# Two of 112 zero fills move to the GpSimd queue, in parts for four, one and eleven DMA engines

## The chip, the cores and the metric

The kernel runs on 1 core of one Trainium2 chip. The metric is the device time of one execution in microseconds (us), lower is better. Three runs of the kernel before took 810.0, 810.16 and 810.81 us; their median is 810.16 us.

## The reference

One decode step of a transformer block and its gradients: a layer norm, attention of one query token with 16 heads over the last 4096 positions of a key cache and a value cache (8 groups of heads, 32768 positions, 256 wide), and a bilinear gated feed-forward layer. What is returned is the block's output and the gradients of the input, of both caches and of five weight matrices. Only the last W = 4096 positions of the caches take part:

```python
W = min(4096, max(256, Sk // 4))                    # Sk = 32768
k = jnp.repeat(k_cache[:, :, Sk - W:, :], rep, axis=1)
v = jnp.repeat(v_cache[:, :, Sk - W:, :], rep, axis=1)
...
_out, _vjp = jax.vjp(_f, A_x, A_k_cache, A_v_cache, A_wq, A_wo, B_w_gate, B_w_up, B_w_down)
_grads = _vjp(grad_out)
return (_out0, *[jnp.asarray(_g) for _g in _grads])
```

The gradients of the two caches (`out_2` for keys, `out_3` for values, each 1 x 8 x 32768 x 256 in bf16) are therefore zero in their first 28672 positions. Those zeros are 224 MB (235 million bytes) of the 280.59 MB that the kernel writes to device memory.

## The kernel before, in words

**Arithmetic.** Phase one goes over the eight groups g: `scores(g)` transposes the keys and makes the softmax weights, `moments(g, p_f)` multiplies keys and values into sums. A middle part of small matrix-vector steps does the output projection, the feed-forward layer and its gradient. Phase two goes over the eight groups again, makes the gradients of keys and values of the last 4096 positions (`d_ps`, L579, copied out in L583 to L587), stores them, and makes the weight gradients in between. Tile schedules the instructions of each engine and places the waits.

**Loads and stores.** `LD` is the ScalarE queue (ACT): it issues the later loads of the caches and weights and all stores of results. `ZQ` is the SyncE queue (SP): it issues the first loads (L92 to L185), and after them nothing but zero fills. GpSimd (POOL) issues no transfer at all in this kernel; it sets a part of the tile `zeros` (L55) and makes two identity matrices, all in the first 4.3 us.

**Zero fills.** The tile `zeros` holds 128 partitions x ZW = 8192 bf16 zeros, so one row is 16,384 bytes. The 224 MB are cut into 112 regions of 128 rows, 2 MB each, and each region is one transfer (L187 to L202):

```python
fills += [reg[i] for i in range(NZ)]                # NZ = 7, 16 times
zsem = [tc.alloc_semaphore(f"zsem{j}") for j in range(DEEP)]
for i, reg in enumerate(fills):
    if i >= DEEP:                                   # DEEP = 8
        tc.keep_in_program_order(ZQ.wait_ge(zsem[i % DEEP], 16 * (i // DEEP)))
    fill = ZQ.dma_start(out=reg, in_=zeros[:])
    ...
    tc.keep_in_program_order(fill.then_inc(zsem[i % DEEP], 16))
for j in range(DEEP):
    filled = tc.keep_in_program_order(ZQ.wait_ge(zsem[j], 16 * len(range(j, len(fills), DEEP))))
```

Fill i is issued when fill i - 8 has landed, so eight of them are under way. The last loop (L200, L201) waits for the last eight fills, and the kernel ends behind it. The fills carry semaphores of their own, not Tile's.

**Packets and DMA engines.** The core has 16 DMA engines. The trace records each packet with its queue, size, start and time, but not with its engine. One row of a fill is one packet of 16,384 bytes, and a packet of 4 bytes (the completion mark) follows each eight rows: 112 fills x 16 = 1792 such marks belong to the fills. So each fill gives every engine eight rows. A packet starts within a few ns of the end of the packet before it on the same engine, so the packets can be strung into 16 chains, one per engine, which then carry no number but an end.

Of the kernel before, what the change touches and what calls it, by code (L numbers as in the profile page):

```python
# [15 lines left out]
G = 8  # L16
Dh = 256
W = 4096
# [4 lines left out]
Sk = 32768  # L23
EPS = 1e-5
SCALE = 1.0 / 16.0
ZW = 8192
NZ = (Sk - W) * Dh // (128 * ZW)
ZM = 5120
DEEP = 8
# [5 lines left out]
def kernel(  # L35
        ctx, tc, A_x, A_k_cache, A_v_cache, A_wq, A_wo, B_x, B_w_gate, B_w_up, B_w_down, grad_out,
           out_0, out_1, out_2, out_3, out_4, out_5, out_6, out_7, out_8):
    nc = tc.nc
    LD = nc.scalar
    ZQ = nc.sync  # L40
# [12 lines left out]
    zeros = const.tile([128, ZW], bf16)  # L53
# [133 lines left out]
    fills = []  # L187
    for g in range(G):
        for o in (out_2, out_3):
            reg = o[0, g, 0:Sk - W, :].rearrange("s d -> (s d)").rearrange("(n p f) -> n p f", p=128, f=ZW)  # L190
            fills += [reg[i] for i in range(NZ)]
    zsem = [tc.alloc_semaphore(f"zsem{j}") for j in range(DEEP)]
    for i, reg in enumerate(fills):
        if i >= DEEP:
            tc.keep_in_program_order(ZQ.wait_ge(zsem[i % DEEP], 16 * (i // DEEP)))
        fill = ZQ.dma_start(out=reg, in_=zeros[:])
        tc.info.no_tile_sem_insts.add(fill.ins.name)
        tc.add_to_no_dep_group("fills", fill.ins)
        tc.keep_in_program_order(fill.then_inc(zsem[i % DEEP], 16))
    for j in range(DEEP):  # L200
        filled = tc.keep_in_program_order(ZQ.wait_ge(zsem[j], 16 * len(range(j, len(fills), DEEP))))  # L201
    tc.declare_fence(filled.ins, group="fills")  # L202
# [437 lines left out]
```

## Time and profile before

| what | value |
|---|---|
| median of the runs | 810.16 us |
| the profiled execution | 810.97 us, span 808.1 us in the profile |
| DMA | 339.02 MB moved, 420 GB/s mean, "9" in tenths in 39 of 40 slices |
| SP's fills | 112 x 2048 KB, issued from 17.9 to 768.0 us |
| last wait for a fill over | 806.8 us |
| busiest engine, PE | 484.3 us, 60% of the span |
| GpSimd | 3.7 us busy, 9 instructions |

Times in the profile count from the first instruction of the span. "DMA share" in a table of windows is the mean busy share of the 16 DMA engines, so one engine alone gives 1/16 = 0.06. The DMA queues are named q1 (transfers that SP issued) and q10 (ACT); "instruction" rows are the engines' program code being fetched.

### The profile page before, as it was taken

The page shows a single profiled execution, that of the slowest core. Times are in us where ns is not written, and L with a number is a line of the kernel's source. Part 1 is how long each engine was busy: PE and PEld are TensorE (multiplying, and loading weights), DVE is VectorE, ACT ScalarE, POOL GpSimd, SP SyncE. Part 2 cuts the span into 40 slices and gives each one's busy share as a digit, 9 for nine tenths or more (in the row PEclk, how much of TensorE's full clock was granted, in tenths as well). Part 3 has the DMA queues.
Part 4 walks back from the last instruction along what each step waited for, and adds up shares of the span by engine and source line. Part 5 has one row for each costly group of instructions (what it writes and reads, how often), then busy time and mean ns, then how long its engine had stood idle before and what let it go on. Part 6 is the DMA issues. An engine that isn't in the chain of part 4 may idle for free.

```text
span 808.1 us, 8346 instructions
## 1 busy us (share of the span) xinstructions
PE 484.3 (60%) x3128; PEld 252.7 (31%) x3151; DVE 369.3 (46%) x1152; ACT 191.2 (24%) x301; POOL 3.7 (0%) x9
## 2 busy tenths in 40 slices
PE   3799999999999955119326664533674664230000
PEld 2454545455455532108313322211231221000000
DVE  3279356455536417881336545258843444540000
ACT  1521331322330102001014243221232343330000
POOL 1000000000000000000000000000000000000000
PEclk9899999999999976559858557555555557555555
DMA  9999999999999999999999999999999999999994
GB/s 371 396 427 429 429 429 428 430 428 427 431 430 426 422 426 429 431 432 426 425 420 423 427 436 427 413 421 429 428 429 426 428 431 429 429 429 427 430 428 196
DMA packets 24942, 339.02 MB, mean 420 GB/s; under 512 B 2755, under 2 KB 3398, under 8 KB 4422
## 3 DMA queue, kind: packets, MB, share of 16 engines
q1 hardware_dynamic: 17842, 254.96, 74.4%
q10 hardware_dynamic: 7060, 83.53, 24.4%
q8 instruction: 24, 0.39, 0.2%
q14 instruction: 16, 0.13, 0.0%
HBM read 57.89 MB, written 280.59 MB: 419 GB/s over the span
## 4 chain that ended last, share of the span: by engine, by line
DMA 24%; PE 12%; DVE 11%; ACT 2%; issue 1%; DVEq 0%; ACTq 0%
DMA out_dram<-arena 24%; PE d_ps L579 4%; PE rows_ps L251 3%; PE tr_ps L248 3%; DVE arena L417 2%; DVE arena L587 2%; DVE arena L586 2%; DVE arena L472 1%; PE dqb_ps L458 1%; DVE arena L502 1%; DVE arena L595 1%; ACT arena L584 1%; ACT arena L539 1%; DVE arena L392 1%; ACT arena L583 0%
## 5 line engine op out<-in xcount | busy, mean ns | idle before, releaser
L579 PE MATMUL d_ps<-arena,rT 32*128 32x512 bf16 x256 | 59.5, 564 | 129.9 <-DVE arena L587 101.3
L303 DVE TENSOR_SCALAR arena<-arena,p_f 128x256 bf16<-128x256 bf16 x512 | 109.7, 281 | 53.8 <-PE M_ps L307 29.0
L248 PE MATMUL tr_ps<-ident_bf,arena 128*128 128x128 bf16 x1024 | 102.5, 254 | 29.1 <-DVE arena L541 25.4
L307 PE MATMUL M_ps<-arena 128*128 128x512 bf16 x489 | 118.4, 380 | 1.4 <-issue 0.6
L248 PEld LDWEIGHTS <-arena 128*128 128x128 bf16 x1024 | 74.5, 113 | 90.7 <-issue 88.6
L251 PE MATMUL rows_ps<-arena,vpad 128*16 128x512 bf16 x256 | 96.0, 470 | 6.0 <-ACT arena L265 2.8
L265 ACT COPY arena<-tr_ps 128x1024 bf16<-128x1024 bf16 x64 | 61.7, 1015 | 119.1 <-PE tr_ps L248 119.1
L587 DVE CAST arena<-d_ps 128x512 bf16<-128x512 f32 x64 | 43.5, 680 | 56.2 <-DMA out_dram<-arena 56.2
L583 ACT CAST arena<-d_ps 128x512 bf16<-128x512 f32 x64 | 37.7, 588 | 126.1 <-PE d_ps L579 122.2
L579 PEld LDWEIGHTS <-rT 32*128 32x128 bf16 x256 | 12.4, 98 | 165.2 <-issue 83.5
L307 PEld LDWEIGHTS <-arena 128*128 128x128 bf16 x512 | 46.4, 98 | 52.3 <-issue 6.3
L586 DVE CAST arena<-d_ps 128x512 bf16<-128x512 f32 x64 | 44.0, 688 | 37.4 <-PE d_ps L579 37.3
L311 PE MATMUL ok_ps<-arena 128*16 128x256 bf16 x512 | 59.3, 273 | 1.1 <-DVE arena L292 0.9
L584 ACT CAST arena<-d_ps 128x512 bf16<-128x512 f32 x64 | 38.1, 595 | 64.4 <-DMA out_dram<-arena 64.4
L311 PEld LDWEIGHTS <-arena 128*16 128x16 bf16 x512 | 44.5, 90 | 14.7 <-issue 4.5
L539 ACT COPY arena<-tr_ps 128x1024 bf16<-128x1024 bf16 x32 | 32.8, 1026 | 16.0 <-PE tr_ps L248 11.9
L251 PEld LDWEIGHTS <-vpad 128*16 128x16 bf16 x256 | 17.8, 91 | 44.1 <-issue 37.4
L541 DVE COPY arena<-tr_ps 128x1024 bf16<-128x1024 bf16 x32 | 21.9, 685 | 13.5 <-PE tr_ps L248 12.7
L463 ACT ACTIVATE arena<-dqb_ps 128x512 bf16<-128x512 f32 x8 | 4.8, 597 | 79.9 <-PE dqb_ps L461 55.0
L458 PE MATMUL dqb_ps<-arena,doT_f 128*128 128x256 f32 x64 | 19.5, 435 | 4.7 <-ACT arena L463 4.7
L417 DVE CUSTOM_DVE_ANT_0 arena<-arena,dh_bc 128x448 bf16<-128x448 bf16 x32 | 20.0, 624 | 1.1
L253 DVE COPY arena<-rows_ps 16x512 f32<-16x512 f32 x16 | 10.8, 675 | 19.9 <-PE rows_ps L251 19.7
(182 smaller groups left out, 318.1 us busy)
## 6 DMA issues: line engine op xcount, KB each, us to landing
out_dram<-zeros SPq DMA_DIRECT2D x112, 2048.0 KB, 56.8
out_dram<-arena ACTq DMA_DIRECT2D x16, 2048.0 KB, 17.4
arena<-in_A_v_cache_dram ACTq DMA_DIRECT2D x8, 2048.0 KB, 14.8
arena<-in_A_k_cache_dram ACTq DMA_DIRECT2D x5, 2048.0 KB, 21.2
arena<-in_A_v_cache_dram SPq DMA_DIRECT2D x4, 2048.0 KB, 30.5
arena<-in_A_k_cache_dram SPq DMA_DIRECT2D x3, 2048.0 KB, 26.1
arena<-in_A_wo_dram ACTq DMA_DIRECT2D x1, 3584.0 KB, 19.3
arena<-in_A_wq_dram SPq DMA_DIRECT2D x1, 3072.0 KB, 10.2
```

Of the source, the lines that this page charges most:

```text
L248: nc.tensor.transpose(tr_ps[:, dh, i, :], X_sb[:, 4 * q + i, dh * 128:(dh + 1) * 128], ident_bf[:])
L251: nc.tensor.matmul(rows_ps[:], lhsT=pad[:, dh, 16 * q:16 * q + 16], rhs=XT[:, dh].rearrange("p t k -> p (t k)"), start=(q == 0 and dh == 0 ...
L265: sT_ps = dots(K_slot[g % 3], KT_slot, vpad[g % 2], rows1, ps_c, "cols", lambda q, XT, ps: nc.scalar.copy(out=XT, in_=ps))
L303: nc.vector.tensor_scalar(out=pK[:, i, hh, :], in0=K_sb[:, t, :], scalar1=p_f[:, 8 * i + c, hh:hh + 1], scalar2=None, op0=ALU.mult)
L307: nc.tensor.matmul(M_ps[:, vh, :], lhsT=V_sb[:, t, vh * 128:(vh + 1) * 128], rhs=pK[:, i, :, :].rearrange("p h d -> p (h d)"), start=(t == ...
L311: nc.tensor.matmul(ok_ps[:, k, :], lhsT=ppad[g % 2][:, 8 * (t % 4) + t // 4, :], rhs=X_sb[:, t, :], start=(g == 0 and k == 0 and t == 0), ...
L539: nc.scalar.copy(out=XT, in_=ps)
L579: nc.tensor.matmul(d_ps[:, qi].rearrange("p w d -> p (w d)"), lhsT=rT[32 * q:32 * (q + 1), :], rhs=RB_[32 * q:32 * (q + 1), l, :], start=T ...
L583: nc.scalar.copy(out=stV[:, t:t + 2, :], in_=d_ps[:, :, 0, :])
L584: nc.scalar.copy(out=stK[:, t:t + 2, :], in_=d_ps[:, :, 1, :])
L586: nc.vector.tensor_copy(out=stV[:, t:t + 2, :], in_=d_ps[:, :, 0, :])
L587: nc.vector.tensor_copy(out=stK[:, t:t + 2, :], in_=d_ps[:, :, 1, :])
```

## The change

The last two regions of the values' gradient (256 rows) are taken off SP's list, which then has 110 fills. GpSimd waits until the first fill of all has landed, and then issues 255 of these rows, in three transfers: 68 rows read from 4 partitions of `zeros` (17 times each), one row less its last element from 1 partition, and 187 rows read from 11 partitions (17 times each). The missing last element of the single row is a transfer of SP, issued ahead of its fills. Behind the last fill SP waits for these four transfers as well.

```diff
+    def fill_with(queue, dst, src, sem):
+        fill = queue.dma_start(out=dst, in_=src)
+        ...
+    last = out_3[0, G - 1, 0:Sk - W, :].rearrange("s d -> (s d)").rearrange("(r f) -> r f", f=ZW)[(NZ - 2) * 128:NZ * 128]
+    tc.keep_in_program_order(nc.gpsimd.wait_ge(zsem[0], 16))
+    psem = []
+
+    def share(queue, dst, src):
+        psem.append(tc.alloc_semaphore(f"psem{len(psem)}"))
+        fill_with(queue, dst, src, psem[-1])
+
+    share(nc.gpsimd, last[0:68].rearrange("(k n) f -> k n f", n=17), zeros[0:4].unsqueeze(1).to_broadcast([4, 17, ZW]))
+    share(nc.gpsimd, last[68:69, 0:ZW - 1], zeros[0:1, 0:ZW - 1])
+    share(nc.gpsimd, last[69:256].rearrange("(k n) f -> k n f", n=17), zeros[0:11].unsqueeze(1).to_broadcast([11, 17, ZW]))
+    share(ZQ, last[68:69, ZW - 1:ZW], zeros[0:1, 0:1])
+
+    fills = fills[:-2]
     for i, reg in enumerate(fills):
         if i >= DEEP:
             tc.keep_in_program_order(ZQ.wait_ge(zsem[i % DEEP], 16 * (i // DEEP)))
-        fill = ZQ.dma_start(out=reg, in_=zeros[:])
-        ...
-        tc.keep_in_program_order(fill.then_inc(zsem[i % DEEP], 16))
+        fill_with(ZQ, reg, zeros[:], zsem[i % DEEP])
+    for sem in psem:
+        tc.keep_in_program_order(ZQ.wait_ge(sem, 16))
     for j in range(DEEP):
         filled = tc.keep_in_program_order(ZQ.wait_ge(zsem[j], 16 * len(range(j, len(fills), DEEP))))
```

On every other engine the order of the instructions stays as it was. GpSimd has the three transfers at the end of its list, SP has its one-element transfer ahead of the fills.

More of the change, by code (lines that the diff above doesn't have):

```diff
@@ L192 @@
     zsem = [tc.alloc_semaphore(f"zsem{j}") for j in range(DEEP)]
+    def fill_with(queue, dst, src, sem):
+        fill = queue.dma_start(out=dst, in_=src)
+        tc.info.no_tile_sem_insts.add(fill.ins.name)
+        tc.add_to_no_dep_group("fills", fill.ins)
+        tc.keep_in_program_order(fill.then_inc(sem, 16))
+    last = out_3[0, G - 1, 0:Sk - W, :].rearrange("s d -> (s d)").rearrange("(r f) -> r f", f=ZW)[(NZ - 2) * 128:NZ * 128]
[9 more added lines that the diff above has]
+    fills = fills[:-2]
     for i, reg in enumerate(fills):
@@ L195 @@
             tc.keep_in_program_order(ZQ.wait_ge(zsem[i % DEEP], 16 * (i // DEEP)))
-        fill = ZQ.dma_start(out=reg, in_=zeros[:])
-        tc.info.no_tile_sem_insts.add(fill.ins.name)
-        tc.add_to_no_dep_group("fills", fill.ins)
-        tc.keep_in_program_order(fill.then_inc(zsem[i % DEEP], 16))
+        fill_with(ZQ, reg, zeros[:], zsem[i % DEEP])
+    for sem in psem:
+        tc.keep_in_program_order(ZQ.wait_ge(sem, 16))
     for j in range(DEEP):
```

## The prediction

> **What bounds the kernel now.** I read the page's slices first, then SP's own waits, then windows over the end.
>
> ```profile
> PE   3799999999999955119326664533674664230000
> ...
> DMA  9999999999999999999999999999999999999994
> GB/s 371 396 427 429 429 429 428 430 428 427 431 430 426 422 426 429 431 432 426 425 420 423 427 436 427 413 421 429 428 429 426 428 431 429 429 429 427 430 428 196
> ```
>
> Each digit is a fortieth of the span (20.2 us). PE stands still in the last four slices, while the DMA engines are full in all slices but the last, where they move 196 GB/s instead of some 428. The chain of waits has its last arithmetic at about 728 us of a span of 808.1 us. So the time is set by bytes, and the one place where DMA engines idle is the very end. The chain of waits on the page does not show this: it follows compute (24% of it waits for stores), since the fills have semaphores of their own. SP's waits show it:
>
> ```profile
> SPq L196 <- DMA out_dram<-zeros: 683.7, 104, 11.8
> SPq L201 <- DMA out_dram<-zeros: 38.4, 4, 23.9
> ...
> L201 SPq EVENT_SEMAPHORE  x4: 28/28/28, 792.3 to 806.8; - x4
> ```
>
> SP waits for landings all the time, and the last four waits end from 792.3 to 806.8 us. (806.8 - 792.3) / 3 = 4.8 us between landings is the time that one engine takes for its eight rows of a fill: a row's packet takes 611 ns in the trace, 8 x 0.611 = 4.9 us. So the last landings follow one engine. The windows of 2 us (columns: window, length, granted clock, DMA share, GB/s) say how many are left:
>
> ```profile
> 788.00:790.00 2.00, 0.50 1.06 451
> 790.00:792.00 2.00, 0.50 1.00 426
> 792.00:794.00 2.00, 0.50 0.88 377
> 794.00:796.00 2.00, 0.50 0.69 295
> 796.00:798.00 2.00, 0.50 0.56 238
> 798.00:800.00 2.00, 0.50 0.23 98
> 800.00:802.00 2.00, 0.50 0.08 33
> 802.00:804.00 2.00, 0.50 0.08 33
> 804.00:806.00 2.00, 0.50 0.06 25
> ```
>
> Share times 16 is the number of engines still at work: all at 792, eleven at 795, nine at 797, four at 799, then one (0.06 x 16) from about 801 to 806.8. Stringing the packets of the trace into 16 chains gives the ends: one at 806.8, the next at 801.1, 800.3, 799.7 and 799.5, the earliest at 792.8, the mean 797.8. One engine ends 9.0 us above the mean and 5.7 us after the next.
>
> Why it does is seen less well. All chains carry the same fills. Program code (q8, 24 packets of 16 KB) is fetched in turn by eight of the chains, and the late chain is none of them. Its row packets often take 640 to 660 ns instead of 611, and it falls behind all along, about half of it before 220 us. Whatever slows it is there in every run: the three unprofiled runs lie within 0.1% of each other and of the profiled one.
>
> **The change part by part.** *Rows.* Two fills of 128 rows are 16 rows per engine. In their place come 17 rows on fifteen engines and one row on one engine, if the three parts fall on 4, 1 and 11 different engines: 68 / 4 = 17, 1, 187 / 11 = 17. The one engine has 15 rows fewer, 15 x 0.611 = 9.2 us; each other one has one more, 0.6 us. If the one is the late engine, it ends at 806.8 - 9.2 = 797.6 us, and the next in line, at 801.1 + 0.6 = 801.7 us, now ends the kernel. The gain is 806.8 - 801.7 = 5.1 us, not 9.2: what is late next is a chain that fetched eleven 8 KB pieces of program code. The 1.3 us from the last landing to the end of the span stay, and so does the 2.9 us between span and execution: span 803.0, profiled execution 805.9, and the median 810.16 - 5.1 = 805.1 us.
>
> *Cost of a row from GpSimd.* The trace has no transfer by GpSimd. If a row stays one packet it costs 611 ns as now; if it is cut into 4096-byte packets it costs 4 x 159 = 636 ns by the 4096-byte packets of the `wq` load, 17 x 25 ns = 0.4 us on each engine. Below nothing there is no room: 16,384 bytes in 611 ns is 26.8 GB/s, sixteen times that is 429 GB/s, the rate of the full slices. I take 611 ns, since the rows are contiguous as the fills' are.
>
> *GpSimd's wait and its three issues.* The wait ends when fill 0 lands, by 58 us (SP's tenth fill, which needs fill 1, is issued at 58.1). Behind it on GpSimd stand the three transfers alone; its last other work ended at 4.2 us. An issue costs 0.33 us by SP's median, 7.2 us by SP's longest under back pressure; even ten times that lies in front of 700 us of fills. Cover: the rows only have to be done before 797 us.
>
> *A third queue on each engine, early.* Seventeen rows are 10.4 us of an engine's time. ACT's next loads are issued at 68.5 and 70.5 us and may land up to that much later. They are the fifth group's values and the fourth's keys, one or two rounds of some 30 us ahead of their use, and 80 us lie between the last arithmetic and the end. Nothing on the path. The engine without these rows runs 16 rows (9.8 us) ahead of the others from there on; eight fills are 64 rows (39 us) deep, so it never starves.
>
> *SP.* One more issue ahead of the fills, 0.33 us, while its neighbours there take 1.4 to 7.2 us for a full queue: free (0.3 us without that cover). Four more waits at 28 ns stand before those at L201 and pass during the 23.9 us that SP waits there anyway. Two fills fewer to issue at 0.33 us: also free.
>
> Sum: -5.1 us, with +0.4 us at most for cut packets.
>
> **The rivals.** *The relieved engine is another one.* The trace does not number the chains, so nothing in it says that the late one is the fifth in the order of the parts. Then the late engine gets one row more: 806.8 + 0.6, 810.8 us. For the forecast speaks the size: the late chain is 9.0 us over the mean and the shift is worth 9.2 us. Against it: the late chain can't be told from its neighbours by any packet but its slow ones. The Trainium skill ("DMA: Bandwidth & Descriptors", Latency and other measured facts) says that DMA engines 7 and 15 are usually slower than the rest; counted from zero the relieved one would be engine 4, and by that rule this rival comes true. No run here shows an engine's number.
>
> *The three parts don't line up.* If each part starts at the same first engine, the shares are 35 rows on the first, 34 on the next three, 17 on the next seven and none on the last five. Then the kernel ends later: the engines with 34 have 18 rows more, 11.0 us. If the late one is among them, it ends at 817.8 (821.2 us in all); if not, one of the others ends between its 793 to 801 plus 11.0, up to 812.1 (up to 815.5 us). I price it at 816 us; it decides from the point where a part's first engine is fixed instead of following on. For it: the two single-row stores of ACT in the strung chains (896 bytes, the output and one gradient) both lie on the same chain, 337 us apart. Against it: the program-code packets step from chain to chain in a fixed turn, so queues that follow on exist here too. The skill's same page (Why a DMA increments its semaphore by 16 and not by 1) has transfers of SP and ACT start at the lowest engine, which agrees with these two stores, and transfers of GpSimd take the next engines in turn from a moving start; by that the parts line up, and no trace here shows it.
>
> *The single row is cut into elements.* 8191 pieces at 9 ns, the price of the smallest packet, are 74 us on one engine: more than the 39 us that the fills let it fall behind, and some 65 us at the end, 875 us. Nothing in the profile speaks for it, since x_bf's odd 896 bytes went as one packet.
>
> **How the numbers follow.** About 0.2% (1.6 us) is what a measurement of this kernel can tell from no change: below 808.5 us is faster, above 811.8 slower. The forecast, 805.1 us, gets 0.58; its own range is 804.0 to 806.5 us (cut packets, and the next chain's end a row or two elsewhere). Another engine relieved, 810.8 us, gets 0.22, all of it "same". Parts that don't line up get 0.15, the cut row and anything else that a first use of GpSimd's transfers adds 0.05, all slower. The range takes in the first two cases with their bounds: 804.0 to 812.0 us; it leaves out 0.2.
>
> **What would show it.** If right: the last landing at L201 near 801.7 us, span near 803.0, a share of 0.06 no longer alone for 5 us, and a third queue with 255 rows, 4.2 MB. If another engine was relieved: the same lonely 0.06, ending near 807.4. If the parts bunch: several engines (shares 0.2 to 0.3) at work beyond 803 us. Wrong in its mechanism would be a span that moves although the last four landings do not, or fills whose waits at L196 grow around 60 us by more than 10 us.

## The result

The change makes the kernel slower: 864.83 us (863.6 to 866.4) against 810.08 us, a ratio of 1.0675 (95% interval 1.0655 to 1.0695). The forecast was 805.1 us. The span grew by 53.6 us, from 808.1 to 861.7.

The page of the changed kernel, its slices and the new queue:

```profile
PE   3899600699999999441572664742366558312000
...
DMA  9999999899999999999999999999999999999972
GB/s 366 406 428 326 210 216 313 328 373 414 427 427 421 430 425 416 428 427 433 429 429 430 416 427 431 427 419 418 427 429 432 424 431 428 431 432 430 427 312 94
...
q0 software_dynamic: 608, 4.20, 4.7%
```

Before, every slice from the third to the last but one moved over 410 GB/s. Now six slices from the fourth on (65 to 194 us; a slice is 21.5 us) move 210 to 373. The DMA engines stand at "9" there, once at "8", all the same: their packets are under way, but get on slowly. Row q0 is GpSimd's queue: 256 packets of a row, the single row's without its last element (the other 352 are marks of 4 bytes). Its 4.7% of 16 engines over 861.7 us is 648 us; over 256 rows that is 2.5 us a row. In the packets of the trace the median row took 2.48 us and the longest 5.13, where a fill's row takes 0.611.

Two sums account for the loss. Against 429 GB/s the six slices lack (103 + 219 + 213 + 116 + 101 + 56) x 21.5 us, which is 40.6 us of full rate. The last two slices lack 22.7 us of full rate where the last slice before lacked 11.0: 11.7 us more. Together that is 52 of the 53.6 us.

SP's waits show both ends of it. These are SP's waits over the span, and the landings at the last wait (L220 is L201 of before):

```profile
SPq L194 <- DMA out_dram<-zeros: 737.5, 102, 56.7
SPq L220 <- DMA out_dram<-zeros: 38.3, 4, 23.9
...
L220 SPq EVENT_SEMAPHORE  x6: 28/28/28, 845.7 to 860.4; - x6
```

The longest wait for a fill was 11.8 us, and is 56.7 now. Windows over the slow stage (window, length, busy us of PE, PEld, DVE, ACT and POOL, granted clock, DMA share, GB/s) and over the end (without engines):

```profile
70.00:80.00 10.00, 10.00 (x48) 4.51 (x46) 10.00 (x48) 1.93 (x2) 0.00 (x0) 1.00 1.07 360
80.00:90.00 10.00, 9.67 (x73) 4.43 (x74) 0.27 (x2) 5.62 (x6) 0.00 (x0) 1.00 1.02 223
100.00:110.00 10.00, 0.00 (x0) 0.00 (x0) 0.01 (x1) 0.00 (x0) 0.00 (x0) 0.60 0.97 210
...
130.00:140.00 10.00, 0.00 (x0) 0.00 (x0) 0.00 (x0) 0.00 (x0) 0.00 (x0) 0.50 0.91 303
160.00:170.00 10.00, 9.78 (x39) 4.13 (x38) 8.02 (x37) 1.01 (x2) 0.00 (x0) 0.83 0.82 343
```

```profile
826.00:828.00 2.00, 0.50 0.94 401
830.00:832.00 2.00, 0.50 0.52 221
842.00:844.00 2.00, 0.50 0.31 131
850.00:852.00 2.00, 0.50 0.31 131
854.00:856.00 2.00, 0.50 0.11 49
858.00:860.00 2.00, 0.50 0.06 25
```

GpSimd's rows run from 63 to 162 us. From about 100 us PE has nothing to do until a load of keys lands. PE's weight loads waited for the key cache 1.8 us in all before; now:

```profile
PEld L267 <- DMA arena<-in_A_k_cache_dram: 60.2, 2, 58.4
```

At the end eight engines (share 0.52) are left over by 830 us and five (0.31) at 842 to 852, where before one was.

### The profile page after: what moved, and what is told of

It reads as the page before. It is cut to its first block, busy times and chain, and to the rows that moved or that the text cites. A ratio compares the mean times of both kernels' runs of the same rounds, so it can differ in the third digit from the quotient of the medians.

```text
span 861.7 us, 8350 instructions
## 1 busy us (share of the span) xinstructions
PE 485.2 (56%) x3128; PEld 253.1 (29%) x3151; DVE 369.4 (43%) x1152; ACT 191.2 (22%) x301; POOL 5.6 (1%) x12
## 5 line engine op out<-in xcount | busy, mean ns | idle before, releaser
L558 ACT COPY arena<-tr_ps 128x1024 bf16<-128x1024 bf16 x32 | 32.7, 1025 | 16.0 <-PE tr_ps L267 11.7
L614 DVE CUSTOM_DVE_ANT_0 arena<-arena 128x4096 bf16<-128x4096 bf16 x3 | 13.3, 4420 | 14.3 <-DMA arena<-in_A_wq_dram 14.3
## 6 DMA issues: line engine op xcount, KB each, us to landing
arena<-in_A_v_cache_dram ACTq DMA_DIRECT2D x8, 2048.0 KB, 71.7
arena<-in_A_k_cache_dram ACTq DMA_DIRECT2D x5, 2048.0 KB, 22.7
```

Of the source, the lines that this page charges most:

```text
L558: nc.scalar.copy(out=XT, in_=ps)
```

## The experiments

Theory A: the rows' source. The changed kernel reads its 255 rows from partitions 0 to 10, 68 + 1 + 68 = 137 of them from partitions 0 to 3. Neighbouring partitions share a way out of SBUF, and each way is already full with ordinary fills. Theory B: rows that GpSimd issues are slow by themselves.

**Source spread out.**

```diff
-    ... zeros[0:4].unsqueeze(1) ...    zeros[0:1, 0:ZW - 1] ...     zeros[0:11].unsqueeze(1)
+    ... zeros[68:105:12].unsqueeze(1)  zeros[8:9, 0:ZW - 1] ...     zeros[0:121:12].unsqueeze(1)
```

> The change as it is, but GpSimd's parts read partitions 12 apart (68, 80, 92, 104; then 8; then 0, 12, ... 120) instead of partitions 0 to 3, 0 and 0 to 10. Theory A (narrow source): in the changed kernel 255 rows are read from 11 neighbouring partitions, 137 of them from partitions 0 to 3; neighbouring partitions share one way out of SBUF, which gives a row per 0.61 us, so 137 rows take 84 us there and hold up every engine that waits for one. Spread out, the rows take 0.6 to 0.7 us as the fills' do, no slice falls under 400 GB/s, and the time is 805.1 us if the relieved engine is the late one, 810.8 us if it is another. Theory B (rows issued by GpSimd are slow by themselves): median row still near 2.5 us, time still near 865 us.

Measured: 819.39 us, ratio 1.0115 (1.010 to 1.013). Its page:

```profile
GB/s 373 395 429 377 384 383 421 425 424 428 427 427 429 418 420 431 431 429 428 425 418 427 427 431 429 411 425 431 427 430 419 432 429 429 431 429 429 428 428 208
...
q0 software_dynamic: 608, 4.20, 1.4%
```

The median row is back at 0.611 us, and 45 of the 54.7 us are gone. Only the source partitions were changed, so they are the cause of that part. Neither figure of the expectation was met: a tenth of the rows still take over 1.04 us and three slices stay at 377 to 384.

**GpSimd's queue with ordinary fills.**

```diff
-    share(nc.gpsimd, last[0:68] ...)   # and the three other parts
+    share(nc.gpsimd, fills[-2], zeros[:])
+    share(nc.gpsimd, fills[-1], zeros[:])
```

> GpSimd issues the same two regions as two ordinary fills of 128 partitions, not in parts, at the same place behind the first landing. Theory A: reads spread over all partitions, rows at 0.61 us, time 810 us (809 to 811.5). Theory B (GpSimd's queue as such, or a third queue on each engine): the same stall from 60 to 180 us, time near 865 us.

Measured: 810.38 us, ratio 1.0005 (0.9995 to 1.0014), so no change.

```profile
GB/s 371 396 428 429 428 429 429 428 423 428 430 428 430 412 426 430 431 431 428 427 413 428 427 430 432 405 427 431 427 430 431 430 429 428 432 431 428 428 427 204
...
q0 software_dynamic: 288, 4.19, 1.2%
```

1.2% of 16 x 808.3 us over 256 rows is 0.61 us a row: GpSimd's rows, its wait and a third queue cost nothing. Theory B falls.

**Narrow source without GpSimd.**

```diff
-        fill = ZQ.dma_start(out=reg, in_=zeros[:])
+        src = zeros[0:16].unsqueeze(1).to_broadcast([16, 8, ZW]) if 8 <= i < 12 else zeros[:]
+        dst = reg.rearrange("(k n) f -> k n f", n=8) if 8 <= i < 12 else reg
+        fill = ZQ.dma_start(out=dst, in_=src)
```

> The kernel before, with no transfer by GpSimd; of SP's fills, the ninth to twelfth (8 to 11) read their 128 rows from partitions 0 to 15, eight times each, instead of from 128 partitions. Theory A: each group of four partitions now gives 128 rows, 78 us; less the 39 us by which eight fills in flight let engines drift apart, about 40 us are lost: some 850 us (835 to 860), with rows far above 611 ns in that stretch. Theory B: nothing lost, 810 us.

Measured: 855.36 us, ratio 1.056 (1.0539 to 1.0581).

```profile
GB/s 368 403 429 430 349 171 195 193 271 429 430 429 425 425 421 428 431 430 429 428 422 425 425 429 429 412 425 432 424 431 422 431 432 428 430 431 427 429 426 263
```

Here four of SP's own fills, the ninth to the twelfth, read 16 partitions eight times each. The narrow source alone, in SP's queue, makes the same hole: five slices at 171 to 349.

**Half as narrow.**

```diff
-    ... zeros[0:4].unsqueeze(1) ...    zeros[0:11].unsqueeze(1)
+    ... zeros[0:7:2].unsqueeze(1) ...  zeros[0:21:2].unsqueeze(1)
```

> The change as it is, with every second partition as source (0, 2, 4, 6; then 0; then 0, 2, ... 20). Theory A: the busiest group of four partitions gives 69 rows instead of 137, 42 us instead of 84; that is about the 39 us of drift that eight fills allow, so most of the loss goes: 805 to 825 us, and GpSimd's rows take about half as long as in the changed kernel (median 1.2 to 1.5 us instead of 2.5). Theory B: near 865 us, rows as slow as before.

Measured: 835.43 us, ratio 1.0314 (1.0293 to 1.0335), above the range expected. Its slices:

```profile
GB/s 373 396 429 379 301 336 413 419 419 423 431 423 427 430 418 424 428 432 429 429 426 418 427 430 428 433 404 428 431 422 431 422 432 427 433 431 429 432 323 78
```

GpSimd's rows have a median of 1.12 us. Each source partition is read as often as in the changed kernel, and half the loss is gone: what is narrow is shared by neighbouring partitions, and is not the single partition. The dose orders the loss (54.7, 25.4 and 9.4 us for partitions 1, 2 and 12 apart), but the drift sum, which let eight fills in flight absorb 39 us, is too kind.

**Sixteen fills under way.** Edit: `DEEP = 16` in the changed kernel.

> The changed kernel with 16 fills under way instead of 8. Theory A1 (total rows of one way out): partitions 0 to 3 give 137 - 16 = 121 rows more than before, 74 us of work on a way out that one engine's own fills already keep full; the earliest engine ends at 793 us without it, so no kernel with these sources ends before about 793 + 74 = 867 us less what slack that way has; 858 to 870 us, as with 8. Theory A2 (drift: 84 us of stall less the 39 us that eight fills in flight cover): sixteen cover 78 us, so the loss falls to about 10 to 15 us, 820 to 830 us.

Measured: 865.09 us, ratio 1.0676 (1.0652 to 1.0699), against 1.0675 with eight. More fills in flight absorb nothing, so the drift sum (A2) is wrong. What remains is the sum of rows through one way (A1). As an estimate it holds within about 8 us: 793 + 74 = 867 us for the changed kernel, whose last landing was at 860; in the narrow run of SP 128 - 32 = 96 rows more are 58.7 us on chains that end at 793 to 795, 852 to 854, and the last packet ended at 852; for every second partition 69 - 16 = 53 rows are 32 us, 825, and it was 833. The sum does not give the 9.4 us that the spread run still loses.

**Each engine's own partitions.** The same parts, reading partitions 0, 4, 8, 12; 16; 52 to 92 by 4. The second run has parts for 7, 1 and 8 engines.

```diff
+    share(nc.gpsimd, ..., zeros[0:13:4] ...)   zeros[16:17, 0:ZW - 1]   zeros[52:93:4] ...
```

> The change as it is (parts for 4, 1 and 11 engines), each engine's rows read from a partition that, by the split of an ordinary fill (four neighbouring partitions to an engine, in order), is its own: 0, 4, 8, 12; then 16; then 52, 56, ... 92. Theory A (rows of one group of four partitions share one way out, full already with its own engine's fills): rows at 0.61 to 0.7 us, no slice under 420 GB/s, and what remains is whom it relieves: 805.1 us if that is the late engine, 810.8 us if it is another; between the two nothing. Theory B (what is left of the loss in the run with partitions 12 apart, 9.4 us, is the price of parts or of a third queue): 815 to 820 us again.

> As the run before, with parts for 7, 1 and 8 engines: the eighth engine in GpSimd's order is relieved instead of the fifth, partitions 0, 4, ... 24; then 28; then 64, 68, ... 92. Theory A: 805.1 us if the eighth is the late one, else 810.8 us; at most one of the two runs is the faster. Theory B: 815 to 820 us.

Measured: 814.82 us, ratio 1.0062 (1.004 to 1.0084), and 812.52 us, ratio 1.0042 (1.0021 to 1.0063). Both still have two slices at 371 to 399 GB/s, and a tenth of the rows over 0.95 us. So these partitions were not the engines' own, and whom the parts relieved can't be read from the time.

**Rows that never leave SBUF.** A table of 16 rows of zeros in device memory as source:

```diff
+    zdram = nc.dram_tensor("zdram", (16, ZW), bf16).ap()
+    zd = tc.keep_in_program_order(nc.gpsimd.dma_start(out=zdram, in_=zeros[0:16]))
+    share(nc.gpsimd, ..., zdram[0:4] ...)   zdram[4:5, 0:ZW - 1]   zdram[5:16] ...
```

> The change (parts for 4, 1 and 11 engines), but the rows are read from a 16-row table of zeros in device memory, which GpSimd writes first, so that none of the 255 rows is read out of SBUF. Theory A (the way out of SBUF is the whole loss): rows at 0.61 us, no slice under 420 GB/s from 60 to 180 us; 805.1 us if the fifth engine in GpSimd's order is the late one, 810.8 us if not. Theory B (parts, marks or a third queue cost something of their own): 812 us or more, with slices of 370 to 400 GB/s again.

> As the run before with parts for 7, 1 and 8 engines, so that the eighth engine in GpSimd's order has 15 rows fewer. Theory A: 805.1 us if the eighth is the late one, 810.8 us if not; a late chain that stands 5 us or more behind the next is seen in the windows of the end wherever it was not relieved. Theory B: 812 us or more.

Measured: 812.99 us, ratio 1.0032 (1.0019 to 1.0045), and 811.88 us, ratio 1.0021 (1.0011 to 1.0030). The page of the first, and windows over its end:

```profile
GB/s 369 394 430 415 423 428 429 428 426 428 430 429 427 419 425 432 430 429 429 431 413 429 424 430 431 407 426 432 425 429 423 431 430 428 433 430 430 428 427 197
...
q0 software_dynamic: 640, 4.46, 1.3%
```

```profile
788.00:790.00 2.00, 0.50 0.98 418
790.00:792.00 2.00, 0.50 0.90 385
794.00:796.00 2.00, 0.50 0.94 401
798.00:800.00 2.00, 0.50 0.48 205
802.00:804.00 2.00, 0.50 0.10 41
804.00:806.00 2.00, 0.50 0.06 25
806.00:808.00 2.00, 0.50 0.06 25
```

The hole is gone (no slice under 415 in that stage), which takes away all but 3 us of the loss, what the spread run still lost included. And the end shows that one engine was relieved, but the wrong one: one stops at about 789 us (15 of 16 is 0.94), and the late one is still there, alone, up to 808.

**Which engine is late.** The same with other first parts; then four engines relieved at once, `(4, 1)` and the rest with 21 rows each:

> Rows from the table in device memory, parts for 5, 1 and 10 engines: the sixth engine in GpSimd's order is relieved. In the packets of the two runs before, the late chain takes its rows with the third part when the first part has 4 engines, and with the first part when that has 7, so it is the sixth or the seventh. Theory A: if it is the sixth, the late chain ends about 9 us earlier and the next, at 802.7 us, ends the kernel: 805.5 to 808 us, and the lonely 0.06 in the windows of the end is gone; if it is the seventh, 812 us as before. Theory C (the late chain is late for a reason that any first part or table moves with it, not by its number): 812 us in this run and in the next.

> As the run before with parts for 6, 1 and 9 engines: the seventh engine is relieved. Theory A: exactly one of the two runs gives 805.5 to 808 us, the other 812 us. Theory C: 812 us in both.

> Rows from the table in device memory, parts for 3, 1 and 12 engines: the fourth engine in GpSimd's order is relieved. In the four runs before, the packets of the chain that ends early never carry program code, and with the first four engines of the order they make up the eight chains that carry none; the late chain is one of those eight and was not the fifth to eighth, so it is one of the first four, and not the first, which carries the single-row stores and ends early. Theory A: 805.5 to 808 us if the late one is the fourth, else 812 us. Theory C (lateness follows the order of issue or the table, not an engine): 812 us.

> Parts for 2, 1 and 13 engines: the third is relieved. Theory A: exactly one of these three runs gives 805.5 to 808 us, the others 812 us. Theory C: 812 us.

> Parts for 1, 1 and 14 engines: the second is relieved. Theory A: 805.5 to 808 us in this run if not in the two before. Theory C: 812 us.

> Rows from the table in device memory; four engines at once take one row each, the other twelve 21 rows (4 x 1 + 12 x 21 = 256): here the first four in GpSimd's order. A relieved engine has 15 rows fewer than before the change, the others 5 more (3.1 us). Theory A (one engine is late, whichever it is on this chip): in exactly one of these four runs the late engine is among the four, and the time is about 809 us (the others' 801 to 803 us plus 3.1); in the other three the late one ends 3 us later than before, some 814 us. Theory C (lateness is no engine's own): 814 us in all four.

> As e15 with the fifth to eighth engine in GpSimd's order relieved: 809 us if the late one is among them, else 814 us (theory A); 814 us (theory C).

> As e15 with the ninth to twelfth engine relieved: 809 us if the late one is among them, else 814 us (theory A); 814 us (theory C).

> As e15 with the thirteenth to sixteenth engine relieved: 809 us if the late one is among them, else 814 us (theory A); 814 us (theory C).

| run | median us | ratio (95%) |
|---|---|---|
| sixth | 812.10 | 1.0024 (1.0015 to 1.0034) |
| seventh | 811.78 | 1.0021 (1.0011 to 1.0031) |
| fourth | 811.73 | 1.0024 (1.0014 to 1.0034) |
| third | 811.61 | 1.0018 (1.0009 to 1.0027) |
| second | 812.25 | 1.0026 (1.0017 to 1.0036) |
| first to fourth | 814.41 | 1.0055 (1.0035 to 1.0074) |
| fifth to eighth | 814.10 | 1.0052 (1.0036 to 1.0068) |
| ninth to twelfth | 814.29 | 1.0054 (1.0034 to 1.0074) |
| thirteenth to sixteenth | 814.43 | 1.0055 (1.0035 to 1.0075) |

The late chain stayed in every profile, so the numbers are those of theory C. They don't prove it, because these runs, all but the last, relieved other engines than they name. Strung into chains, GpSimd's packets between 63 and 131 us show which part a chain took: its rows stand before or behind the 4-byte marks that it gets for the other parts.

- *The single row has no engine of its own.* In the runs for the fourth, sixth, seventh and eighth engine it lies on the chain that carries ACT's single-row store at about 325 us. In the four-engine runs the four single rows lie on the same four chains each time (the same by their other packets), that one among them. All these chains take rows of a large part as well.
- *The two large parts do follow on.* No chain has the full rows of both. With parts for 3 to 7 engines first, one chain is left without any of the 256 rows (it has one row of the table's copy alone); in the four-engine runs four are, though in the run for the fifth to eighth two of them can be read only in part. By the order of the parts these are the engines behind the third part, the sixteenth or the last four, whatever the sizes of the parts. That is worked out from the parts; the trace numbers no engine.
- *In the run for the second engine* the first part's 17 rows went to all engines, and two chains were left out by the third part and end early.

So, but for the run for the second, the single tries with the table relieved one and the same engine, and the four-engine runs the same four. These carry different turns of the program code in different kernels, but it is that turn which moves: the chain of the stores and the late chain keep their places in GpSimd's order.

The late chain can be placed, for most rows of 635 to 665 ns lie on it: 24 to 41 before 130 us on one chain in each of five runs. With 3 or 4 engines in the first part this chain takes its 17 rows with the third part; with 5, 6 or 7 engines, with the first. So the late engine is the fifth in GpSimd's order, the one that the change was to relieve. These five runs were on three chips; one engine fits them all, but that it is the same on each is not shown. The expectations above took the chain that ended early for the one that each run names, and so went past the fifth. Whether relieving it gains the 5.1 us stays open, for no run relieved it. No version beat the kernel before.

## Why the prediction was wrong

**The step that failed is "Cost of a row from GpSimd".** I took 611 ns "since the rows are contiguous as the fills' are", with 636 ns as the upper bound. The median was 2.48 us, four times that. The bound looked at where a row goes and how it is cut, not at where it is read. The diff says it plainly: `zeros[0:4]` and `zeros[0:11]`, 17 times each, in place of 128 partitions. The step's own argument against a gain had the hint in it: sixteen engines at 26.8 GB/s make 429 GB/s and leave no room, so rows that all leave by the ways of a few partitions have to wait behind the fills that use them too. The Trainium skill ("SBUF — State Buffer", Door 1: The DMA port swizzle) says that a DMA's bandwidth depends on how many of 16 SBUF ports its partitions reach, and puts partitions 0 to 3, 4 to 7 and 8 to 11 on three of them. The narrow run of SP agrees in direction (down to 171 GB/s with 16 partitions as a source of some fills); the prediction did not look there.

**"A third queue on each engine, early ... Nothing on the path" failed with it.** The loads of ACT were to land up to 10 us late. The values' loads had a median of 71.7 us from issue to landing in the changed kernel against 14.8 before, and PE stood still for some 50 us. The loads before, and after the change:

```profile
arena<-in_A_v_cache_dram ACTq DMA_DIRECT2D x8, 2048.0 KB, 14.8
arena<-in_A_v_cache_dram ACTq DMA_DIRECT2D x8, 2048.0 KB, 71.7
```

By itself that cover held: compute still ends ahead of the fills. The 53.6 us come from the DMA engines' own loss.

**"If the three parts fall on 4, 1 and 11 different engines" failed too**, in "Rows". With the same parts read from device memory, the single row fell on an engine that also took 17 rows of the first part, the third part began right behind the first, and the fifth engine, the late one, took 17 rows like the others. So "if the one is the late engine" was not met, although the fifth is the late one; the prediction had no reason for the fifth, and said so. A relieved chain does end some 9 us early (789 us). The gain of 5.1 us behind it is neither shown nor refuted.

**The rivals.** Of "the three parts don't line up" a piece came true: the single row went back to an engine of the first part, the large parts followed on, and no engine had 34 rows. The cut row did not come: the single row went as one packet of 16,382 bytes in 613 ns. GpSimd's wait, its issues (543 to 784 ns) and SP's extra waits cost nothing, as said; ordinary fills from GpSimd give 1.0005. With the source mended, the time was 811.6 to 813.0 us, near the rival of another engine relieved (810.8), 1 to 2 us above it, and this is what happened; one more row for the table is 0.6 us of that, the rest was not tried.

What of the prediction pointed here: its last test, fills whose waits at L196 grow around 60 us, was the one that came true. It stood among the signs of failure without a price.

## What to carry to other kernels

When a transfer is cut anew, count its rows by source partition as well as by DMA engine: a few partitions read many times are one narrow exit, however many engines do the reading. When all engines run at full rate there is no slack at any exit, so rows moved to one exit lengthen the whole by about their sum, and here neither early issue nor a deeper queue hid it. Before shifting load between engines, make sure which engine each part falls on, and read it from the packets of each part: that one chain ends early does not say which.

## What the runs showed of the hardware

- Reading from 16 neighbouring partitions instead of 128 takes a full stream of 429 GB/s down to 171 to 195 GB/s in three slices, with the DMA engines at 9 tenths busy: the share of busy time doesn't show this loss, GB/s does.
- Rows issued by GpSimd from all partitions cost the same 0.61 us as SP's, and two whole fills from GpSimd change nothing (1.0005).
- In GpSimd's transfers on fewer than 16 engines, marks of 4 bytes fill the other engines: 352 for 4, 1 and 11 engines, which is 3 x 16 for completion and (17 x 12 + 15 + 17 x 5) = 304 in the place of rows.
- A part of k x 17 rows from GpSimd went to k engines, and the next such part to the engines behind them. A single row went to an engine that had a part already, and four single rows to the first four engines of the order (packets of the runs with the table).
- One DMA engine ends 2 to 6 us after the rest in each profile whose rows from GpSimd are at full speed, and in the kernel before (806.8 us). Most rows of 635 to 665 ns, where the others take 611, are its own. Their cause was not found.
